# First loads of a gated linear-attention and SwiGLU kernel: two x tiles on two queues, the halves of wk on the other queue each

## The chip, the core and the metric

The kernel runs on one core of a Trainium2 chip. TensorE (PE) does the matmuls, VectorE (DVE), ScalarE (ACT) and GpSimd (POOL) the elementwise work, and SyncE (SP) issues DMAs. ACT can issue DMAs as well. The metric is the device time of one execution in microseconds, lower is better.

## What is computed

Two branches of one input x (2048 tokens, 512 features, bf16) are mixed by a gate. Branch A is linear attention with 32 heads of 16 features, without a causal mask; branch B is a SwiGLU block with 1376 hidden features. Cut to what matters:

```python
g = sigmoid((x * gate_w).sum(-1, keepdims=True))
# branch A
q, k, v = split_heads(x @ wqkv)
pq, pk = phi(q), phi(k)          # phi(t) = where(t > 0, t + 1, exp(t)) + 1e-6
kv  = einsum("bhsd,bhse->bhde", pk, v)
z   = einsum("bhsd->bhd", pk)
a   = (pq @ kv) / (pq @ z + 1e-6) @ wo
# branch B
b   = (silu(x @ w1) * (x @ w3)) @ w2
out = g * a + (1 - g) * b
```

## The kernel before

The tokens are cut into 16 tiles of 128 (`t`), and four tiles make a block of 512 (`tb`). The feature dimension of 512 is cut into four chunks of 128 (`kc`). All weights and all of x stay on chip: `x_sb` holds x with tokens on the partitions, `xT` holds it transposed (features on the partitions), and `wk_sb`, `wq_sb`, `wv_sb`, `w1_sb`, `w3_sb`, `w2_sb`, `wo_sb` hold the weights.

The work comes in this order on TensorE, and the order is written out by hand (line 152 puts TensorE under manual scheduling, so its instructions run in the order of the program text):

1. Warm matmuls (`emit_warm`, lines 160 to 167): six with 512 columns and three with 128, on constants, whose result is not used.
2. Transposes of x tiles 0 and 1 (`emit_xT`, lines 171 to 183): four 128x128 transposes a tile. DVE copies the first two of a tile out of PSUM (line 181), ACT the other two (line 183).
3. The k projection of the first block (lines 376 to 385). Its sixteen matmuls (line 186) run in a fixed order. The first six are, as (kc, t): (0,0), (1,0), (0,1), (1,1), (2,0), (3,0). So the first four need only chunks 0 and 1 of wk, and the fifth is the first to need chunks 2 and 3. Then come (2,1), (3,1), and tiles 2 and 3.
4. For the tiles from 4 on, the k projection alternates with `emit_xp` (line 206), which accumulates x^T phi(k) over all tokens.
5. The q projection of block 0, the products that fold kv and wo into one matrix `W_sb`, and then, block by block, the SwiGLU matmuls (`emit_ffn`), the next block's q projection and remainder, and the output (`emit_out`).

xT of tiles 0 and 1 is made on TensorE as said. xT of all other tiles comes by transposing DMAs from DRAM (lines 89 and 93).

The DMAs are issued in the order of the text on their queue. SP's queue (`dq`) carries nearly all of them: x tiles 0 and 1 (line 84), the second half of wk (line 86), the transposing load of tiles 2 and 3 (line 89), then the rest of xT and x, and the weights in the order of use (lines 92 to 114). ACT's queue carries one: the first half of wk (line 85). After it ACT runs a one-element `Exp` (line 88, tile `pre`), ahead of which the table of activation functions is loaded. Scheduling of ACT, DVE, POOL and SP is left to the framework.

x tiles 0 and 1 are loaded in one DMA of 256 KB whose partition p takes rows 2p and 2p + 1 of x (2 KB in one piece). So tile 0 holds the even rows of the first 256 and tile 1 the odd ones. The sums over tokens do not depend on the order, and the output rows of these two tiles are stored with the same stride (`out_first`, lines 83 and 371).

The lines that matter here:

```python
dq.dma_start(out=x_sb[:, 0:TF, :], in_=x_first)
nc.scalar.dma_start(out=wk_sb[:, 0:2, :], in_=wqkv_r[:, 0:2, D : 2 * D])
dq.dma_start(out=wk_sb[:, 2:4, :], in_=wqkv_r[:, 2:4, D : 2 * D])
pre = consts.tile([1, 1], FP32, name="pre")
nc.scalar.activation(out=pre[:], in_=nc.const_aps.tensor(0.0, [1, 1], FP32), func=ACT.Exp)
```

Of the kernel before, what the change touches and what calls it, by code (L numbers as in the profile page):

```python
# [8 lines left out]
ACT = mybir.ActivationFunctionType  # L9
ALU = mybir.AluOpType  # L10
AX = mybir.AxisListType
ENG = mybir.EngineType
FP32 = mybir.dt.float32
# [4 lines left out]
def kernel(  # L18
# [12 lines left out]
    nc = tc.nc  # L31
    P = nc.NUM_PARTITIONS

    Bb, S, D = A_x.shape
# [5 lines left out]
    TB = 512  # L40
    NTB = S // TB
    TPB = TB // P
    FC = F // P
    FR = F - FC * P
    FM = FC * P
# [3 lines left out]
    x2d = A_x.flatten_outer_dims()  # L49
    out2d = out.flatten_outer_dims()  # L50
# [13 lines left out]
    x_sb = consts.tile([P, NT, D], BF16, name="x_sb")  # L64
    xT = consts.tile([P, KC, S], BF16, name="xT")
    wk_sb = consts.tile([P, KC, D], BF16, name="wk_sb")
# [5 lines left out]
    w2_sb = consts.tile([P, FC, D], BF16, name="w2_sb")  # L72
# [3 lines left out]
    wqkv_r = A_wqkv.rearrange("(kc d) n -> d kc n", d=P)  # L76
    w1_r = B_w1.rearrange("(kc d) f -> d kc f", d=P)
    w3_r = B_w3.rearrange("(kc d) f -> d kc f", d=P)
    x_r = x2d.rearrange("(t p) d -> p t d", p=P)
    dq = nc.sync  # L80
    TF = 2
    x_first = x2d[0 : TF * P, :].rearrange("(p j) d -> p j d", j=TF)
    out_first = out2d[0 : TF * P, :].rearrange("(p j) d -> j p d", j=TF)
    dq.dma_start(out=x_sb[:, 0:TF, :], in_=x_first)
    nc.scalar.dma_start(out=wk_sb[:, 0:2, :], in_=wqkv_r[:, 0:2, D : 2 * D])
    dq.dma_start(out=wk_sb[:, 2:4, :], in_=wqkv_r[:, 2:4, D : 2 * D])
    pre = consts.tile([1, 1], FP32, name="pre")
    nc.scalar.activation(out=pre[:], in_=nc.const_aps.tensor(0.0, [1, 1], FP32), func=ACT.Exp)
    dq.dma_start(
        out=xT[:, :, TF * P : TB], in_=x2d[TF * P : TB, :], transpose=True  # L90
    )
    for tb in range(1, NTB):
        dq.dma_start(
            out=xT[:, :, tb * TB : (tb + 1) * TB], in_=x2d[tb * TB : (tb + 1) * TB, :],
# [7 lines left out]
    with nc.allow_non_contiguous_dma(reason="one gate weight per partition and chunk"):  # L102
        dq.dma_start(
            out=wr_sb[:, :, 2 * FR : NR], in_=gate_w.rearrange("(kc d o) -> d kc o", d=P, o=1)
# [3 lines left out]
        dq.dma_start(out=w1_sb[:, :, fsl], in_=w1_r[:, :, fsl])  # L108
        dq.dma_start(out=w3_sb[:, :, fsl], in_=w3_r[:, :, fsl])
    dq.dma_start(out=wo_sb[:], in_=A_wo.rearrange("(kc d) n -> d kc n", d=P))  # L110
    w2_r = B_w2[0:FM, :].rearrange("(fc f) d -> f fc d", f=P)
    for fcs in (slice(0, FC // 2), slice(FC // 2, FC)):
        dq.dma_start(out=w2_sb[:, fcs, :], in_=w2_r[:, fcs, :])
    dq.dma_start(out=w2r_sb[:FR, :], in_=B_w2[FM:F, :])

    pk_sb = consts.tile([P, NT, D], BF16, name="pk_sb")
# [5 lines left out]
        out=bm, in_=bm, pattern=[[-Dh, HPC], [0, Dh]], compare_op=ALU.is_ge, fill=0.0,  # L122
# [3 lines left out]
        out=bm, in_=bm, pattern=[[Dh, HPC], [0, Dh]], compare_op=ALU.is_ge, fill=0.0,  # L126
# [33 lines left out]
    def emit_warm(*widths):  # L160
        warm = psX.tile([P, TB], FP32, tag="XP3", name="warm")
        for n in widths:
            nc.tensor.matmul(  # L163
                warm[:, 0:n], lhsT=warm_l, rhs=warm_r[:, 0:n], start=True, stop=True
            )

    emit_warm(TB, TB, TB, TB, TB, TB, P, P, P)

    st = {}

# [163 lines left out]
    def emit_out(tb, tt):  # L334
        t = tb * TPB + tt
        tsl = slice(tt * P, (tt + 1) * P)

        if t < NT - 1:
            parts = [(0, D, True)]
        else:  # L340
            h, q3 = D // 2, 3 * D // 4
            parts = [(0, h, True), (h, q3, False), (q3, D, True)]
        o_out = work.tile([P, D], BF16, tag="o_out", name="o_out")
        lo = 0
        for i, (a, b, store) in enumerate(parts):
            o_ps = psX.tile([P, b - a], FP32, tag=f"XP{2 + (tt + i) % 2}", name="o_ps")
            for c in range(KC):
                nc.tensor.matmul(  # L348
                    o_ps[:], lhsT=st[tb, "pqT"][:, c, tsl], rhs=W_sb[:, c, a:b],
                    start=(c == 0), stop=False,  # L350
                )
            nc.tensor.matmul(  # L352
                o_ps[:], lhsT=st[tb, "hTr"][:FR, tsl], rhs=w2r_sb[:FR, a:b],
                start=False, stop=False,
            )
            for fc in range(FC):
                nc.tensor.matmul(  # L357
                    o_ps[:], lhsT=st[tb, "hT"][:, fc, tsl], rhs=w2_sb[:, fc, a:b],
                    start=False, stop=(fc == FC - 1),
                )  # L360
            if i < 2:
                nc.scalar.activation(  # L362
                    out=o_out[:, a:b], in_=o_ps[:], func=ACT.Copy, scale=omg[:, t : t + 1]
                )
            else:
                nc.vector.tensor_scalar(  # L366
                    out=o_out[:, a:b], in0=o_ps[:], scalar1=omg[:, t : t + 1], scalar2=None,
                    op0=ALU.mult,
                )
            if store:  # L370
                rows = out_first[t] if t < TF else out2d[t * P : (t + 1) * P, :]
                nc.sync.dma_start(out=rows[:, lo:b], in_=o_out[:, lo:b])
                lo = b


# [39 lines left out]
    for c in range(KC):  # L415
# [7 lines left out]
        out=kvT_sb[:], in0=kvT_ps[:],  # L423
# [21 lines left out]
    for tb in range(NTB):  # L445
        for fc in range(FC if tb == 0 else 0, FC):
            emit_ffn(tb, fc)
        nx = tb + 1
        for tt in range(TPB):
            if nx < NTB:  # L450
                emit_q(nx, tt, psX, "XP0")
                if tt % 2 == 0:
                    emit_rem(nx, tt // 2, psX, "XP1")
            emit_out(tb, tt)
            if nx < NTB:
                emit_den(nx, tt)
        if nx < NTB:
            emit_norm(nx)
# [30 lines left out]
```

## Time and profile before

| What | Value |
|---|---|
| Median of 4 runs | 179.52 us (179.37 to 180.15) |
| Profiled execution, its own time | 179.57 us |
| Its span, first to last instruction | 177.7 us |
| TensorE busy | 173.9 us, 98% of the span |
| First transpose of x starts | 3.93 us |
| First k matmul starts | 4.75 us |
| Last matmul starts | 174.61 us |

A profile is of one execution. Times in it count from the first instruction, so the span is a little shorter than the execution's own time; here 1.87 us lie around it. "PE" is a matmul, "PEld" a weight load that overlaps it. "SPq" and "ACTq" are DMAs being issued by SP and ACT: the length given is that of the issue, and the time to landing is told apart, in the view of the DMA issues. What stands in square brackets at the end of a timeline line is the engine's idle time before it and what ended that.

### The profile page before, as it was taken

To read this page: it belongs to the slowest core of one execution; us is meant where nothing else is said; L and a number is where in the kernel's file an instruction comes from. 1 tells how busy PE (TensorE), PEld (TensorE's weight loads), DVE (VectorE), ACT (ScalarE), POOL (GpSimd) and SP (SyncE) were. 2 spreads that over 40 slices of the span, in tenths; PEclk is the share of its full clock that TensorE was granted. 3 is DMA by queue.
4 is the path that set the end of the run, shared out by engine and by line. 5 is a ranking of instruction groups with operands and counts; after the bars stand their busy time and mean duration, and the time that the engine had idled before them with its cause. 6 is when DMAs were issued, how large, how long until landed. Compare 5 with 4: busy or idle time off the path is not lost.

```text
span 177.7 us, 2469 instructions
## 1 busy us (share of the span) xinstructions
PE 173.9 (98%) x884; PEld 84.0 (47%) x884; DVE 117.9 (66%) x203; ACT 66.0 (37%) x124; POOL 63.3 (36%) x71
## 2 busy tenths in 40 slices
PE   8999999999999999999999999999999999999993
PEld 3444444474444444444454544444545444444463
DVE  0596857898998637498776366978754668775000
ACT  3634224466443434333244333243434323241211
POOL 5197655967262323262003232710032328000000
PEclk9999999999999999999999999999999999999999
DMA  5999999921014011124000111230002022200011
GB/s 170 236 293 239 246 339 363 348 78 28 9 30 90 3 41 38 40 59 89 0 0 11 39 35 37 70 79 6 0 7 66 7 70 59 59 0 0 30 41 51
DMA packets 30252, 15.14 MB, mean 85 GB/s; under 512 B 20672, under 2 KB 30112, under 8 KB 30240
## 3 DMA queue, kind: packets, MB, share of 16 engines
q1 hardware_dynamic: 29968, 14.72, 30.6%
q10 hardware_dynamic: 272, 0.26, 0.4%
q8 instruction: 7, 0.11, 0.3%
q14 instruction: 5, 0.04, 0.1%
HBM read 8.42 MB, written 2.10 MB: 59 GB/s over the span
## 4 chain that ended last, share of the span: by engine, by line
PE 98%; DVE 0%; issue 0%; DVEq 0%
PE o_ps L357 19%; PE gate_ps L312 19%; PE up_ps L320 19%; PE o_ps L348 8%; PE XP L206 8%; PE q_ps L219 8%; PE k_ps L186 6%; PE r_ps L243 3%; PE o_ps L352 2%; PE k L186 2%; PE warm L163 2%; PE xTp L176 1%; PE kvT_ps L418 1%; PE W_ps L440 0%; DVE o_out L366 0%; PE z_ps L431 0%
## 5 line engine op out<-in xcount | busy, mean ns | idle before, releaser
L312 PE MATMUL gate_ps<-xT,w_sb 128*128 128x512 bf16 x160 | 41.1, 379 | 0.0
L320 PE MATMUL up_ps<-xT,w_sb 128*128 128x512 bf16 x160 | 41.1, 379 | 0.0
L227 POOL TENSOR_TENSOR qz<-pq,z_sb 128x512 f32<-128x512 bf16 x16 | 18.5, 1165 | 59.6 <-DVE pq L147 58.4
L325 ACT ACTIVATE th<-gate_ps 128x512 bf16<-128x512 f32 x40 | 23.9, 597 | 37.9 <-PE gate_ps L312 37.5
L357 PE MATMUL o_ps<-w_sb,hT 128*128 128x512 bf16 (+2 forms) x180 | 37.5, 355 | 0.0
L327 DVE SCALAR_TENSOR_TENSOR gs<-th,gate_ps 128x512 bf16<-128x512 bf16 x40 | 27.3, 683 | 5.6 <-ACT th L325 5.3
L330 DVE TENSOR_TENSOR hT<-up_ps,gs 128x512 bf16<-128x512 f32 x40 | 27.7, 691 | 3.8
L144 DVE TENSOR_SCALAR phi_m<-phi_e 128x512 bf16<-128x512 bf16 x32 | 14.2, 442 | 21.3 <-ACT phi_e L142 21.2
L357 PEld LDWEIGHTS <-hT 128*128 128x128 bf16 x180 | 16.8, 97 | 17.9
L320 PEld LDWEIGHTS <-w_sb 128*128 128x128 bf16 x160 | 15.7, 98 | 18.9
L312 PEld LDWEIGHTS <-w_sb 128*128 128x128 bf16 x160 | 15.6, 98 | 18.6
L362 ACT ACTIVATE o_out<-o_ps,omg 128x512 bf16<-128x512 f32 (+2 forms) x17 | 11.2, 657 | 30.4 <-PE o_ps L357 30.4
L292 POOL TENSOR_TENSOR pqn<-pq,rden 128x512 bf16<-128x512 bf16 x16 | 16.6, 1058 | 14.0 <-DVE rden L285 11.7
L196 POOL TENSOR_TENSOR pks<-pks,pk_sb 128x512 f32<-128x512 f32 x15 | 17.4, 1162 | 7.3 <-DVE pk_sb L147 6.7
L348 PE MATMUL o_ps<-W_sb,pqT 128*128 128x512 bf16 (+2 forms) x72 | 16.8, 355 | 0.0
L230 DVE TENSOR_REDUCE den<-qz 128x32 f32<-128x512 f32 x16 | 11.0, 685 | 8.6 <-POOL qz L227 8.5
L219 PE MATMUL q_ps<-wq_sb,xT 128*128 128x512 bf16 x64 | 16.4, 379 | 0.0
L206 PE MATMUL XP<-pk_sb,x_sb 128*128 128x512 bf16 x64 | 16.3, 379 | 0.0
L142 ACT ACTIVATE phi_e<-k_ps 128x512 bf16<-128x512 f32 x12 | 7.2, 597 | 14.4 <-PE k_ps L186 14.4
L142 ACT ACTIVATE phi_e<-q_ps 128x512 bf16<-128x512 f32 x16 | 9.6, 598 | 7.8 <-PE q_ps L219 7.8
L186 PE MATMUL k_ps<-wk_sb,xT 128*128 128x512 bf16 x48 | 12.3, 379 | 0.0
L147 DVE SCALAR_TENSOR_TENSOR pq<-q_ps,phi_m 128x512 bf16<-128x512 f32 x16 | 11.1, 691 | 0.5
(59 smaller groups left out, 117.7 us busy)
## 6 DMA issues: line engine op xcount, KB each, us to landing
w_sb<-in_B_w_dram SPq DMA_DIRECT2D x6, 640.0 KB, 8.4
out_dram<-o_out SPq DMA_DIRECT2D x15, 128.0 KB, 1.9
x_sb<-in_A_x_dram SPq DMA_DIRECT2D x2, 512.0 KB, 4.2
x_sb<-in_A_x_dram SPq DMA_DIRECT2D x1, 768.0 KB, 5.1
wq_sb<-in_A_wqkv_dram SPq DMA_DIRECT2D x1, 512.0 KB, 6.1
wv_sb<-in_A_wqkv_dram SPq DMA_DIRECT2D x1, 512.0 KB, 6.7
wo_sb<-in_A_wo_dram SPq DMA_DIRECT2D x1, 512.0 KB, 10.0
wk_sb<-in_A_wqkv_dram ACTq DMA_DIRECT2D x1, 256.0 KB, 3.6
```

Source lines behind the costliest of these rows:

```text
L186: nc.tensor.matmul(k_ps[:], lhsT=xT[:, kc, t * P : (t + 1) * P], rhs=wk_sb[:, kc, :], start=(kc == 0), stop=(kc == KC - 1),)
L196: nc.gpsimd.tensor_add(pks[:], pks[:], pk_sb[:, t, :])
L206: nc.tensor.matmul(XP_ps[dc][:], lhsT=x_sb[:, t, dc * P : (dc + 1) * P], rhs=pk_sb[:, t, :], start=(t == 0), stop=(t == NT - 1),)
L219: nc.tensor.matmul(q_ps[:], lhsT=xT[:, kc, ts_tok], rhs=wq_sb[:, kc, :], start=(kc == 0), stop=(kc == KC - 1),)
L227: nc.gpsimd.tensor_tensor(out=qz[:], in0=st[tb, "pq"][:, tt, :], in1=z_sb[:], op=ALU.mult)
L312: nc.tensor.matmul(gate_ps[:], lhsT=w1_sb[:, kc, fsl], rhs=xT[:, kc, tok_sl], start=(kc == 0), stop=(kc == KC - 1),)
L320: nc.tensor.matmul(up_ps[:], lhsT=w3_sb[:, kc, fsl], rhs=xT[:, kc, tok_sl], start=(kc == 0), stop=(kc == KC - 1),)
L325: nc.scalar.activation(out=th[:], in_=gate_ps[:], func=ACT.Tanh, scale=0.5)
L327: nc.vector.scalar_tensor_tensor(out=gs[:], in0=th[:], scalar=1.0, in1=gate_ps[:], op0=ALU.add, op1=ALU.mult)
L330: nc.vector.tensor_tensor(out=st[tb, "hT"][:, fc, :], in0=up_ps[:], in1=gs[:], op=ALU.mult)
L348: nc.tensor.matmul(o_ps[:], lhsT=st[tb, "pqT"][:, c, tsl], rhs=W_sb[:, c, a:b], start=(c == 0), stop=False,)
L357: nc.tensor.matmul(o_ps[:], lhsT=st[tb, "hT"][:, fc, tsl], rhs=w2_sb[:, fc, a:b], start=False, stop=(fc == FC - 1),)
```

## The change

x tiles 0 and 1 become two loads of 128 KB, tile 0 on SP's queue and tile 1 on ACT's; tile t holds rows 128t to 128t + 127 again. The first half of wk moves to SP's queue, behind x tile 0. The second half of wk moves to ACT's queue and stands behind the one-element `Exp`, and so behind the load of its table; these few instructions are put under manual scheduling for ACT, so that they keep this order. Two of the three short warm matmuls go. w2 is loaded by one DMA instead of two. The outputs of tiles 0 and 1 are stored to contiguous rows, like all others.

```diff
-    x_first = x2d[0 : TF * P, :].rearrange("(p j) d -> p j d", j=TF)
-    out_first = out2d[0 : TF * P, :].rearrange("(p j) d -> j p d", j=TF)
-    dq.dma_start(out=x_sb[:, 0:TF, :], in_=x_first)
-    nc.scalar.dma_start(out=wk_sb[:, 0:2, :], in_=wqkv_r[:, 0:2, D : 2 * D])
-    dq.dma_start(out=wk_sb[:, 2:4, :], in_=wqkv_r[:, 2:4, D : 2 * D])
     pre = consts.tile([1, 1], FP32, name="pre")
-    nc.scalar.activation(out=pre[:], in_=nc.const_aps.tensor(0.0, [1, 1], FP32), func=ACT.Exp)
+    with tc.manual_schedule(engines={ENG.Activation}):
+        dq.dma_start(out=x_sb[:, 0, :], in_=x_r[:, 0, :])
+        nc.scalar.dma_start(out=x_sb[:, 1, :], in_=x_r[:, 1, :])
+        dq.dma_start(out=wk_sb[:, 0:2, :], in_=wqkv_r[:, 0:2, D : 2 * D])
+        nc.scalar.activation(
+            out=pre[:], in_=nc.const_aps.tensor(0.0, [1, 1], FP32), func=ACT.Exp
+        )
+        nc.scalar.dma_start(out=wk_sb[:, 2:4, :], in_=wqkv_r[:, 2:4, D : 2 * D])
...
-    w2_r = B_w2[0:FM, :].rearrange("(fc f) d -> f fc d", f=P)
-    for fcs in (slice(0, FC // 2), slice(FC // 2, FC)):
-        dq.dma_start(out=w2_sb[:, fcs, :], in_=w2_r[:, fcs, :])
+    dq.dma_start(out=w2_sb[:], in_=B_w2[0:FM, :].rearrange("(fc f) d -> f fc d", f=P))
...
-    emit_warm(TB, TB, TB, TB, TB, TB, P, P, P)
+    emit_warm(TB, TB, TB, TB, TB, TB, P)
...
-                rows = out_first[t] if t < TF else out2d[t * P : (t + 1) * P, :]
-                nc.sync.dma_start(out=rows[:, lo:b], in_=o_out[:, lo:b])
+                nc.sync.dma_start(
+                    out=out2d[t * P : (t + 1) * P, lo:b], in_=o_out[:, lo:b]
+                )
```

## Prediction

> **What bounds the kernel now.** I read the page's busy shares first, then the chain that ended last, then the timeline of the first 12 us in narrow windows, then the DMA issues, and last when each loaded tile is first used.
>
> ```profile
> span 177.7 us, 2469 instructions
> PE 173.9 (98%) x884; PEld 84.0 (47%) x884; DVE 117.9 (66%) x203; ACT 66.0 (37%) x124; POOL 63.3 (36%) x71
> ...
> PE 98%; DVE 0%; issue 0%; DVEq 0%
> ```
>
> TensorE is busy for 173.9 of 177.7 us and is the whole chain. The chain in order of time has no gap from 3.93 us to the last matmul. So an edit counts only if it moves the moment at which the dense stream begins, or opens a hole in it; DVE, ACT and POOL have room everywhere. The last matmul starts at 174.61 us, and what follows (one eviction, one store) is not touched. All of the decision lies in the first six microseconds:
>
> ```profile
> 0.80 0.45 ACTq L85 DMA_DIRECT2D wk_sb<-in_A_wqkv_dram  x1
> 0.81 0.40 SPq L84 DMA_DIRECT2D x_sb<-in_A_x_dram  x1
> 0.84 3.04 PE L163 MATMUL warm<-const-bfloat16-1.0 128*128 128x512 bf16 x9 [0.84 <-PEq L473]
> 1.27 0.41 SPq L86 DMA_DIRECT2D wk_sb<-in_A_wqkv_dram  x1
> 1.28 1.28 ACT L88 ACT_TABLE_LOAD   x1 [1.28 <-PEq L473]
> 1.73 1.32 SPq L89 DMA_TRANSPOSE xT<-in_A_x_dram  x1
> 2.58 0.20 ACT L88 ACTIVATE pre<-const-float32-0.0 1x1 f32<-1x1 f32 x1
> 3.92 0.77 PEld L176 LDWEIGHTS <-x_sb 128*128 128x128 bf16 x8 [0.31 <-DMA x_sb<-in_A_x_dram]
> 4.57 0.79 ACT L183 ACTIVATE xT<-xTp 128x256 bf16<-128x256 bf16 x2 [1.79 <-PE xTp L176]
> 4.75 3.64 PE L186 MATMUL k<-wk_sb,xT 128*128 128x512 bf16 x16
> ```
>
> The columns are start and length in us. Three things are to be seen. The transposes wait for x: it lands 3.1 us after its issue (0.81 + 3.1 = 3.9). The warm matmuls were done before that: the last one starts at 3.57. And the sixteen k matmuls begin once the transposes are through, at 4.75. The DMA view gives the two halves of wk:
>
> ```profile
> wk_sb<-in_A_wqkv_dram ACTq DMA_DIRECT2D x1, 256.0 KB, 3.6
> x_sb<-in_A_x_dram SPq DMA_DIRECT2D x1, 256.0 KB, 3.1
> wk_sb<-in_A_wqkv_dram SPq DMA_DIRECT2D x1, 256.0 KB, 4.0
> ```
>
> So half one (kc 0, 1) lands at 0.80 + 3.6 = 4.4, half two (kc 2, 3) at 1.27 + 4.0 = 5.27. By the order written out, half one is first needed by k matmul 1 (4.75) and half two by k matmul 5, which starts at 5.64: slack 0.35 and 0.37 us.
>
> **The clock of the start.** TensorE is slow here. The 512-column warm matmuls start 0.43 us apart and the transposes 0.107 us apart; later 512-column matmuls start 0.216 us apart.
>
> ```profile
> 4.75 0.41 PE L186 MATMUL k<-wk_sb,xT 128*128 128x512 bf16 x1
> ...
> 4.75 0.62 PE L186 MATMUL k<-wk_sb,xT 128*128 128x512 bf16 x2
> ```
>
> Both lines are narrow windows: the first holds k matmul 1 alone (0.41 us, the settled ones take 0.379), the second 1 and 2, so 2 starts at 5.00, 0.243 after 1. With c us of the 0.243 at the slow pace, c/0.427 + (0.243 - c)/0.216 = 1 gives c = 0.055: the fast pace begins at about 4.81 us. (The granted clock of the rows reads 1.00 all along; the spacing is what shows it.) I take 4.81 as fixed in time, since the changed kernel keeps TensorE busy from 0.84 on as well.
>
> **The change, part by part.**
>
> Warm matmuls: nine become seven, two of 128 columns go. The seventh starts at 3.360, so the transposes can begin at 3.360 + 0.107 = 3.47, if x tile 0 is there; before they began at 3.93. At most 0.46 us is won.
>
> x as two 128 KB loads, one on each queue, issued where x and wk half one are issued now (0.81 and 0.80). No row shows a 128 KB load. Bounds: 1.9 us (the 128 KB stores of the DMA view) and 3.6 us (the ACT queue's load). Tile 0 lands between 2.7 and 4.4, tile 1 likewise. I take 3.1 us or a little less for tile 0 and 3.1 for tile 1, because together they are the same 256 KB that took 3.1 now, with nothing ahead of them. Tile 0 is needed at 3.47, tile 1 four transposes later, at 3.47 + 4 x 0.107 = 3.90, which is 0.80 + 3.1. The eight transposes then end at 4.32. At the far bound (tile 1 at 4.4) the transposes end near 4.8, k matmul 3 is at 5.26 and not 5.21, and the part costs 0.05 us.
>
> The Trainium skill, "DMA: Bandwidth & Descriptors", section "Issuing engines are not separate DMA queues", speaks against this part: loads from two queues run on the same DMA engines, and only issue time is saved. The busy DMA share of 0.99 to 1.10 between 2.75 and 4.25 us agrees. Taken strictly, both tiles land when the one load did, the transposes start at 3.93 and this part is worth nothing: 179.57.
>
> wk half one on the sync queue at 1.27, where half two is now. It comes behind the 256 KB of x, as it does in effect now (both were issued at 0.80, and x landed first), so I keep its landing at 4.4 to 4.45. Bounds: 3.1 and 4.0 us after 1.27, that is 4.4 and 5.27. k matmul 1 starts at about 4.47 and not 4.75.
>
> Then the sum. From 4.47 to 4.81 it runs at 0.427: 0.34/0.427 = 0.80 of it is done, the rest takes 0.20 x 0.216 = 0.04. k matmul 2 starts at 4.85 and not 5.00: **0.15 us won**. The slow clock takes the rest of the 0.28. Matmul 5 starts at 4.85 + 3 x 0.216 = 5.50.
>
> wk half two on ACT, written behind the table load and the dummy activation. It has to land by 5.50 for the gain, and by 5.64 for no loss. Its issue time is the open point. If ACT issues it while the table load runs (from 1.28 on), landing is 1.3 to 1.5 plus 4.0 = 5.3 to 5.5, and nothing stalls. If it waits until the activation starts or ends (2.58, 2.78), landing is 2.58 + 3.6 = 6.2 to 2.78 + 4.0 = 6.8, and TensorE, whose order is fixed by hand, stands still. So this part costs between 0 and 1.15 us against before. I take the early issue: the activation starts 0.01 us after the table load ends, so it had been handed on already while the table load ran, and what stands behind it in ACT's stream is then free to issue. Behind the issue on ACT stand the copies of xT (line 183), first at about 4.1 in the new kernel; even the late issue, 0.45 us long, is over by 3.23.
>
> The skill's "Perfetto Trace Analysis", section "Sequencer Loop", says the same of a sequencer (engine instructions are pushed into a queue); no ACT DMA behind a running instruction is in this trace.
>
> The rest is hidden. On SP the first transposing load stays third (1.73); its tile lands at 6.23, and k matmul 9, which needs it, moves from 6.51 to 6.36, so 0.13 us of slack is left. w2 in one load instead of two: the halves are issued at 25.0 and 26.8 and land within 10.6 us, before 38 us, and w2 is first used at 59.1, a cover of some 20 us; SP has one issue less. The stores of output tiles 0 and 1 are 128 KB as before, near 63 and 66 us, and TensorE does not wait for them. x tiles 0 and 1 hold other rows, in the same shapes.
>
> Sum: profiled execution 179.57 (span 177.7 and 1.87 around it) less 0.15 gives 179.4. The median shown is 179.52, 0.05 lower, which I leave aside.
>
> **Rivals.**
> 1. Nothing won, or a little lost: both x tiles at 3.9, or wk half one late. If half one lands at 4.7 to 5.0, matmul 1 starts there and not at 4.75; matmul 3 was held by the copy of tile 1 until 5.21. Cost 0 to 0.25 us: 179.55 to 179.8. For it: half two, issued at 1.27 on this queue, took 4.0 us. Against it: that one had 512 KB ahead of it.
> 2. wk half two is late (slower). One mechanism: the second ACT issue waits for the table load. From an issue later than about 1.65 (5.64 - 4.0) every microsecond goes straight into the stream, because k matmuls 5 to 16 follow in fixed order. Price 0.55 to 1.15: 180.1 to 180.7, middle 180.4. For it: its place in ACT's order. Against it: the 0.01 us gap.
> 3. The full gain: the fast clock comes earlier along with the work and half one is in time. Then all of the 0.46 is kept: 179.1. Against it: the clock has changed in time, not in work, in the one trace there is.
>
> **How the numbers follow.** A difference of 0.3% (0.54 us) is about what a measurement of this kernel can tell from no change. Forecast 179.4 with 0.50; rival 1 with 0.15; rival 2 with 0.25; rival 3 with 0.10. Forecast and rival 1 lie within 0.3%; rival 2 lies above it except at its lowest end; rival 3 lies inside by 0.08 us, so I split it, half faster. The four runs of before alone go from 179.37 to 180.15, and I add 0.04 to faster and nothing to slower for such scatter: faster 0.09, same 0.66, slower 0.25. The range runs from 179.05 (rival 3 inside) to 180.4 (half of rival 2), which leaves out some 0.17.
>
> **What would show it.** In the changed profile: transposes near 3.47 and k matmul 1 near 4.47; k matmul 2 near 4.85; no hole before k matmul 5; ACT's second DMA issue before 2.5 us. A second ACT issue at 2.6 or later with a hole before matmul 5 is rival 2; transposes at 3.9 are rival 1; fast spacing well before 4.8 is rival 3. A hole later than 8 us would mean that I overlooked a load.

## The result, and the profile after

The change made the kernel slower. The median is 180.14 us (44 executions) against 179.62 us (63 executions of the kernel before, the earlier four among them); the ratio is 1.0033, with a 95% interval of 1.0021 to 1.0044, that is 0.4 to 0.8 us. Ratios here leave out slow executions, those more than 1.5% above the fastest of their kernel. The fastest executions are 0.46 us apart (179.57 and 179.11). Five of the 44 took 181.9 to 182.5 us; none of the 63 took more than 180.42.

The profiled execution of the changed kernel has a span of 178.4 us. This is the timeline of its first microseconds (start, length, engine, line, operation; in brackets the engine's idle time before it and what ended that):

```profile
0.80 0.41 ACTq L85 DMA_DIRECT2D x_sb<-in_A_x_dram  x1
...
0.81 0.40 SPq L84 DMA_DIRECT2D x_sb<-in_A_x_dram  x1
...
1.24 1.28 ACT L87 ACT_TABLE_LOAD   x1 [1.24 <-PEq L474]
1.26 0.42 SPq L86 DMA_DIRECT2D wk_sb<-in_A_wqkv_dram  x1
1.30 0.43 ACTq L90 DMA_DIRECT2D wk_sb<-in_A_wqkv_dram  x1
...
3.49 0.78 PE L176 MATMUL xTp<-ident,x_sb 128*128 128x128 bf16 x8
...
5.32 3.61 PE L186 MATMUL k<-wk_sb,xT 128*128 128x512 bf16 x16 [1.04 <-DMA wk_sb<-in_A_wqkv_dram]
```

The transposes did move forward, from 3.93 to 3.49. But the k matmuls moved back, from 4.75 to 5.32, and the bracket names what they waited for: wk. The second half of wk, which stands behind the table load in ACT's program, was issued at 1.30, while that load was still running (1.24 to 2.52), and so only 0.04 us after the first half on SP. The DMA view (last column: us from issue to landing) gives the landings:

```profile
wk_sb<-in_A_wqkv_dram SPq DMA_DIRECT2D x1, 256.0 KB, 4.0
wk_sb<-in_A_wqkv_dram ACTq DMA_DIRECT2D x1, 256.0 KB, 4.2
...
x_sb<-in_A_x_dram ACTq DMA_DIRECT2D x1, 128.0 KB, 2.8
x_sb<-in_A_x_dram SPq DMA_DIRECT2D x1, 128.0 KB, 2.6
```

Half one now lands at 1.26 + 4.01 = 5.27 us, and half two 0.25 us after it, at 5.52. In the kernel before, the trace has the two landings at 4.45 and 5.25. So the half that is needed first lost 0.8 us. The chain that ended last, in order of time, now begins with that load (start, length, what):

```profile
1.26 4.01 DMA wk_sb<-in_A_wqkv_dram
5.32 3.61 PE k L186 x16
```

One more view shows what the DMA engines did meanwhile. These are the same microsecond of both kernels, first before and then after (length; busy time and instructions of PE, PEld, DVE, ACT, POOL; granted clock; DMA share; GB/s):

```profile
4.25:5.25 1.00, 1.00 (x10) 0.74 (x9) 0.58 (x2) 0.65 (x2) 0.00 (x0) 1.00 1.20 291
```

```profile
4.25:5.25 1.00, 0.02 (x1) 0.10 (x1) 0.24 (x1) 0.49 (x2) 0.00 (x0) 1.00 1.19 271
```

TensorE went from full to empty, and the DMA engines were as busy as before and moved nearly as much (271 against 291 GB/s). The bytes came at much the same rate. They came in another order.

The trace shows the order itself: it lists each packet (a piece of 1 KB for wk) with its queue, start and length. In the kernel before, half two's first packet started at 3.75 us, when 84% of half one's 256 packets were done. In the changed kernel it started at 3.22, when 11% were, and from 3.5 to 4.5 us SP's queue moved 151 KB of half one while ACT's moved 198 KB of half two.

From the first XP matmul (line 206) on, nothing differs: the last matmul of the kernel starts 166.38 us after it in both profiles, to 0.01 us. So the price can be read at one place, the start of that matmul: 8.235 before, 8.765 after, 0.53 us later.

### The profile page after: what moved, and what is told of

It reads as the page before. It is cut to its first block, busy times and chain, and to the rows that moved or that the text cites. A ratio compares the mean times of both kernels' runs of the same rounds, so it can differ in the third digit from the quotient of the medians.

```text
span 178.4 us, 2465 instructions
## 1 busy us (share of the span) xinstructions
PE 173.5 (97%) x882; PEld 83.6 (47%) x882; DVE 117.9 (66%) x203; ACT 65.9 (37%) x124; POOL 63.2 (35%) x71
## 4 chain that ended last, share of the span: by engine, by line
PE 95%; DMA 2%; SPq 0%; DVE 0%; issue 0%; DVEq 0%
PE o_ps L357 19%; PE up_ps L320 19%; PE gate_ps L312 19%; PE o_ps L348 8%; PE XP L206 8%; PE q_ps L219 8%; PE k_ps L186 6%; PE r_ps L243 3%; DMA wk_sb<-in_A_wqkv_dram 2%; PE k L186 2%; PE o_ps L352 2%; PE kvT_ps L419 1%; PE W_ps L441 0%; SPq L84 0%; DVE o_out L366 0%; PE z_ps L432 0%
```

## The experiments

Three readings were to be told apart. **S (sharing):** the halves of wk were now issued on two queues at the same time, ran side by side on the DMA engines, and the first became nearly as late as the second. **Q (queue):** half one is late because it stands second on SP's queue, behind x tile 0. **W:** the fewer warm matmuls or the single load of w2 are what costs.

All landings and starts are in us from the first instruction. Half one and half two are the halves of wk; "T" is the transposing load of tiles 2 and 3; k1 is the start of the first k matmul, XP that of the first XP matmul. "Fast from" is the start of the first stretch of full clock in the trace's clock records; from there on 512-column matmuls start 0.216 us apart and no longer 0.427. (e1's trace has no such record; there the time is worked out from the spacing.) All of these are from the one profiled execution of each run. Times are medians of all executions; the ratio is to executions of the kernel before on the same chip, whose medians were 179.70 (e1 to e4), 179.48 (e5 to e8) and 179.62 (f).

| Run | x landed | half one | half two | T | k1 | fast from | XP | time | ratio (95%) |
|---|---|---|---|---|---|---|---|---|---|
| before | 3.88 | 4.45 | 5.25 | 6.23 | 4.75 | 4.80 | 8.24 | 179.62 | |
| after | 3.44, 3.60 | 5.27 | 5.52 | 6.50 | 5.32 | 3.87 | 8.77 | 180.14 | 1.0033 (1.0021 to 1.0044) |
| e1_half2_sync | 3.83, 3.63 | 4.39 | 6.23 | 7.28 | 4.71 | 6.55 | 9.07 | 180.24 | 1.0030 (1.0011 to 1.0048) |
| e2_half2_waits | 3.44, 3.63 | 6.21 | 9.51 | 9.47 | 6.25 | 4.55, then 14.79 | 14.62 | 184.38 | 1.0228 (1.0184 to 1.0273) |
| e3_swapped | 3.60, 3.77 | 5.65 | 5.41 | 6.59 | 5.69 | 4.90 | 9.14 | 182.55 | 1.0138 (1.0096 to 1.0179) |
| e4_side_edits | 3.66 | 4.35 | 5.47 | 6.52 | 4.44 | 3.87 | 8.30 | 179.67 | 0.9989 (0.9972 to 1.0006) |
| e5_quarter | 3.51, 3.34 | 5.02 | 4.36, 5.53 | 6.69 | 5.06 | 5.96 | 8.94 | 180.57 | 1.0050 (1.0026 to 1.0074) |
| e6_fill | 3.34, 3.52 | 6.04 | 5.36 | 7.00 | 6.08 | 4.90 | 9.53 | 180.48 | 1.0042 (1.0023 to 1.0061) |
| e7_split_T | 3.68 | 4.36 | 5.20 | 5.68, 6.50 | 4.56 | 6.01 | 8.73 | 180.38 | 1.0043 (1.0020 to 1.0066) |
| e8_both_act | 3.55 | 4.25 | 5.16 | 6.15 | 4.34 | 3.68 | 7.93 | 179.95 | 1.0018 (1.0000 to 1.0035) |
| f1_x_1kb | 4.38 | 4.71 | 5.54 | 6.45 | 5.25 | 6.76 | 9.45 | 179.85 | 1.0028 (1.0010 to 1.0046) |
| f2_after_again | 3.49, 3.65 | 5.99 | 6.25 | 7.19 | 6.03 | 4.38 | 9.48 | 180.30 | 1.0063 (1.0033 to 1.0093) |
| f3_before_again | 3.74 | 4.31 | 5.19 | 6.18 | 4.61 | 4.64 | 8.08 | 179.36 | one execution |
| f4_after_fill | 3.48, 3.65 | 4.97 | 5.44 | 6.47 | 5.20 | 5.87 | 8.99 | 180.59 | 1.0052 (1.0033 to 1.0070) |

**e1_half2_sync: half two behind half one on SP.**

```diff
         dq.dma_start(out=wk_sb[:, 0:2, :], in_=wqkv_r[:, 0:2, D : 2 * D])
+        dq.dma_start(out=wk_sb[:, 2:4, :], in_=wqkv_r[:, 2:4, D : 2 * D])
...
-        nc.scalar.dma_start(out=wk_sb[:, 2:4, :], in_=wqkv_r[:, 2:4, D : 2 * D])
```

> The changed kernel, but wk's second half goes on SP's queue right behind the first half, so the two halves no longer run on two queues. Theory S (sharing: in the changed kernel the second half was issued at 1.30 us, ran beside the first half on the same DMA engines and made it late): half one lands at 4.4 to 4.5 us and not 5.27, half two at 5.2 to 5.4, k matmul 1 starts near 4.5 and k matmul 5 near 5.4; time 0.1 to 0.4 us below before, 179.2 to 179.5. Theory Q (queue: half one is late because it now stands second on SP's queue, behind x tile 0): half one still lands near 5.3 and the time stays at that of the changed kernel, 180.1. Theory W (the warm matmuls or w2 are what costs): 180.1 as well, with half one early.

Half one landed at 4.39 and k1 came at 4.71, so S holds and Q falls: half one's place behind x tile 0 was the same. (k1 was not earlier because the x tiles landed only at 3.63 and 3.83 here, and the transposes, at the slow pace, ran until 4.7.) The rest was a miss: half two landed at 6.23, not by 5.4, and the time stayed at 180.24. The timeline and the stages of the profile show what went on (the second fence's columns are those of the stages above):

```profile
1.27 0.44 SPq L86 DMA_DIRECT2D wk_sb<-in_A_wqkv_dram  x1
1.75 0.46 SPq L87 DMA_DIRECT2D wk_sb<-in_A_wqkv_dram  x1
2.26 1.68 SPq L91 DMA_TRANSPOSE xT<-in_A_x_dram  x1
...
4.71 4.53 PE L186 MATMUL k<-wk_sb,xT 128*128 128x512 bf16 x16
```

```profile
4.50:5.50 1.00, 1.00 (x6) 0.50 (x5) 0.40 (x2) 0.77 (x2) 0.00 (x0) 1.00 1.58 185
5.50:6.50 1.00, 1.00 (x4) 0.39 (x3) 0.00 (x0) 0.00 (x0) 0.00 (x0) 1.00 0.83 162
```

The transposing load is now issued fourth, at 2.26 instead of 1.73, and while it ran beside the rest of half two the engines moved 185 and 162 GB/s, against 278 and 273 in the same stages before. T landed at 7.28 instead of 6.23, and the matmul that needs it, the ninth, started at 7.34 instead of 6.51. So the repair of one wait prepared another. No matmul waited for T in this profile, since TensorE was slow until 6.55 and arrived at its ninth matmul no earlier than T. In an execution with an early fast pace it would have had to wait, but none such was traced; how much of the time of e1 is T and how much the clock is not shown.

**e2_half2_waits: half two really behind the table load.** The dummy activation writes one element of wk's second half, which the load then overwrites, so the load has to wait.

```diff
         nc.scalar.activation(
-            out=pre[:], in_=nc.const_aps.tensor(0.0, [1, 1], FP32), func=ACT.Exp
+            out=wk_sb[0:1, 2, 0:1], in_=nc.const_aps.tensor(0.0, [1, 1], FP32), func=ACT.Exp
         )
```

> The changed kernel, but the one-element activation writes into the second half of wk, which the load then overwrites; so the load must wait for the activation and is really behind the table load. Theory S: ACT issues it near 2.75 us, half one has the DMA engines to itself until then and lands at 4.4 to 4.6, k matmul 1 near 4.5; half two lands 2.8 to 4.2 us after its issue, at 5.5 to 6.9, and k matmul 5 starts then (before: 5.64). Time from 0.1 below to 1.2 above before, 179.5 to 180.8, and the hole stands before k matmul 5, not before k matmul 1. Theory Q: half one lands near 5.3 all the same, and the hole before k matmul 1 stays; 180.1 or more.

The issue came where expected, at 2.77. Neither half landed where S expected it. The timeline of TensorE, and three stages of the profile:

```profile
3.49 1.03 PE L176 MATMUL xTp<-ident,x_sb 128*128 128x128 bf16 x8
6.25 1.02 PE L186 MATMUL k<-wk_sb,xT 128*128 128x512 bf16 x4 [1.73 <-DMA wk_sb<-in_A_wqkv_dram]
9.55 5.28 PE L186 MATMUL k<-wk_sb,xT 128*128 128x512 bf16 x12 [2.27 <-DMA wk_sb<-in_A_wqkv_dram]
```

```profile
4.55:7.96 3.41, 1.02 (x4) 0.38 (x4) 0.09 (x1) 0.38 (x1) 0.00 (x0) 1.00 1.15 114
7.96:14.78 6.82, 5.23 (x13) 1.93 (x13) 2.83 (x6) 1.79 (x3) 1.76 (x2) 0.50 1.12 245
14.78:20.00 5.22, 5.17 (x25) 2.35 (x24) 4.15 (x7) 1.79 (x3) 3.40 (x3) 1.00 1.13 238
```

Two things are to be seen. First, half two now met the transposing load instead of half one, on another queue, and the two obstructed each other: 114 GB/s over 3.4 us, T at 9.47, half two at 9.51. Even half one, whose last packet had ended at 3.85, as early as in the kernel before, got its last completion counts only at 6.21. Why the two loads hinder each other so much is not shown. Second, the holes seem to cost the clock: after the stretch of 3.41 us in which TensorE was busy for 1.02, the granted clock (third column from the right) falls to 0.50 from 7.96 to 14.78 us, and the k matmuls run at 0.427 us again. The profiled execution was the longest of six (186.08 us, the others 182.2 to 184.7), so its numbers show what can happen and not the usual price; no other execution of e2 was traced.

**e3_swapped: the halves of wk on each other's queue.**

```diff
-        dq.dma_start(out=wk_sb[:, 0:2, :], in_=wqkv_r[:, 0:2, D : 2 * D])
+        nc.scalar.dma_start(out=wk_sb[:, 0:2, :], in_=wqkv_r[:, 0:2, D : 2 * D])
+        dq.dma_start(out=wk_sb[:, 2:4, :], in_=wqkv_r[:, 2:4, D : 2 * D])
...
-        nc.scalar.dma_start(out=wk_sb[:, 2:4, :], in_=wqkv_r[:, 2:4, D : 2 * D])
```

> The changed kernel with the halves of wk on each other's queue: half one on ACT behind x tile 1, half two on SP behind x tile 0, both issued near 1.25 us. Theory S: they still run side by side, both land at 5.1 to 5.5, k matmul 1 waits until then; 180.0 to 180.2. Theory Q: half one on ACT lands at 4.4, k matmul 1 near 4.5, 179.3 to 179.5.

```profile
wk_sb<-in_A_wqkv_dram ACTq DMA_DIRECT2D x1, 256.0 KB, 4.4
wk_sb<-in_A_wqkv_dram SPq DMA_DIRECT2D x1, 256.0 KB, 4.1
```

```profile
5.69 3.61 PE L186 MATMUL k<-wk_sb,xT 128*128 128x512 bf16 x16 [1.01 <-DMA wk_sb<-in_A_wqkv_dram]
```

S again. Half one, on ACT from 1.24, landed at 5.65, 0.15 us later than S allowed; half two, on SP from 1.27, at 5.41; k1 started at 5.69. Here the halves stand on the queues on which the kernel before has them, and yet they hinder each other. What differs from before is x: with x split over both queues, both halves stand second on their queue and come up together; before, half two stood behind the whole of x. The time was a miss (180.0 to 180.2 was expected): two executions took 180.7 us, the other four 182.4 to 182.9.

**e4_side_edits: the kernel before, with the fewer warm matmuls and the single load of w2.**

```diff
-    emit_warm(TB, TB, TB, TB, TB, TB, P, P, P)
+    emit_warm(TB, TB, TB, TB, TB, TB, P)
...
-    for fcs in (slice(0, FC // 2), slice(FC // 2, FC)):
-        dq.dma_start(out=w2_sb[:, fcs, :], in_=w2_r[:, fcs, :])
+    dq.dma_start(out=w2_sb[:], in_=B_w2[0:FM, :].rearrange("(fc f) d -> f fc d", f=P))
```

> The kernel before with two parts of the change alone: seven warm matmuls instead of nine, and w2 in one load. The loads of x and wk are those of before. Theories S and Q: as before within 0.2 us, 179.4 to 179.8, transposes still at 3.9. Theory W: 0.4 us or more above before, by a later rise of the TensorE pace or a hole after 30 us.

```profile
4.44 4.03 PE L184 MATMUL k<-wk_sb,xT 128*128 128x512 bf16 x16
8.30 1.03 PE L204 MATMUL XP<-pk_sb,x_sb 128*128 128x512 bf16 x4
```

No difference that shows, ratio 0.9989 with 1 inside the interval; W falls. (Lines are two earlier here. The transposes started at 3.71, and not at 3.9 as expected, as x landed at 3.66.) This profile is also the fair partner of the changed kernel's: TensorE became fast at 3.87 in both. The first XP matmul starts at 8.30 here and 8.77 there: 0.46 us.

**e5_quarter: half as much beside half one.** Chunk 2 of wk on SP behind half one, only chunk 3 (128 KB) on ACT.

```diff
         dq.dma_start(out=wk_sb[:, 0:2, :], in_=wqkv_r[:, 0:2, D : 2 * D])
+        dq.dma_start(out=wk_sb[:, 2:3, :], in_=wqkv_r[:, 2:3, D : 2 * D])
...
-        nc.scalar.dma_start(out=wk_sb[:, 2:4, :], in_=wqkv_r[:, 2:4, D : 2 * D])
+        nc.scalar.dma_start(out=wk_sb[:, 3:4, :], in_=wqkv_r[:, 3:4, D : 2 * D])
```

> The changed kernel with half as much on the other queue: chunk 2 of wk goes on SP behind half one, only chunk 3 (128 KB instead of 256 KB) stays on ACT beside half one. Theory S (what is issued early on the other queue shares the DMA engines with half one): a dose, so half one lands between the 4.39 us of the run with nothing beside it and the 5.27 us of the changed kernel, at 4.6 to 5.0, and k matmul 1 starts there. Rival (any load on ACT at that time costs the same, whatever its size): 5.2 to 5.4. The first transposing load is issued 0.4 us later on SP than in the changed kernel, lands at 7.0 or later, and holds k matmul 9 back; so the time is no better than the changed kernel's: 180.0 to 180.4.

With 0, 128 and 256 KB beside it, half one landed at 4.39, 5.02 and 5.27 in these profiles. The order is that of a dose, but the changed kernel's other two profiles have 5.99 and 4.97 for 256 KB, so the steps between are not resolved by single profiles. What stands is that the small load, needed last, came first (4.36). Half one's 5.02 is at the end of what S expected (4.6 to 5.0). T at 6.69 was earlier than expected, and the time, 180.57, above what was expected (180.0 to 180.4). Two of the twelve executions took 182.19 and 182.75.

**e6_fill: e3_swapped with three matmuls in the idle stretch.** Their result is not used.

```diff
     emit_xT(1)
+    emit_warm(TB, TB, TB, tag="XP0")
```

> The kernel with the halves of wk swapped between the queues (its runs: 180.7 twice, 182.4 to 182.9 four times), with three more 512-column matmuls whose result is not used between the transposes and k matmul 1, in the stretch in which TensorE stood idle for 1.1 us. Theory C (clock: the runs near 182.7 are those in which the idle stretch kept TensorE at the slow pace for one more period): no run above 181.3, median 180.5 to 181.1. Rival (a DMA lands 2 us late in these runs): the runs near 182.7 stay, four in six or so.

Nine executions, 179.95 to 180.95, none near 182.7, although half one landed later still in its profile (6.04). So C: the long executions of e3_swapped look like a matter of TensorE's pace after an idle stretch, not of a DMA. (e3 and e6 ran on different chips, and e6's profile still has 0.66 us of idle time before k1.) **f4_after_fill** did the same to the changed kernel, with two matmuls:

> The changed kernel with two more 512-column matmuls without use between the transposes and k matmul 1, in its idle stretch of one microsecond. The loads are those of the changed kernel, so half one still lands near 5.3 and the time stays 0.3 to 0.7 above before. Theory C (clock): the few runs near 182 (5 of 44 of the changed kernel) are gone, none above 181.3. Rival (those runs are a late DMA): one or two of a dozen remain near 182.

Ten executions, 179.83 to 180.98, none near 182, against 8 of 56 of the changed kernel (5 of 44 and 3 of 12 in f2_after_again). The median did not fall, as half one was still late; the two matmuls cost something themselves when TensorE is slow. (Were the share still 8 in 56, ten executions without one would come up one time in five; it is e6_fill that carries the point, nine without where four of six had it.)

No long execution was traced, so the clock is argued here and not seen. Three figures of the record speak for it. Every execution above 181.5 us, but for those of e2, belongs to a kernel whose profile has TensorE idle for 0.5 to 1.5 us before k1 (the changed kernel, e3, e5). One more stretch of 3.41 us, as in e2, at the slow pace would cost about 3.41 x (1 - 0.216/0.427) = 1.7 us, an estimate; e3's long executions took 1.7 to 2.2 more than its short ones. And the mean granted clock of the long ones is 0.997 to 1.00, where e2's executions with a later fall of the clock have 0.98 to 0.99: so it would be the first rise that came late, not a fall after it. The records do not count the slow pace ahead of the first rise.

**e7_split_T: the kernel before with the first transposing load cut in two.**

```diff
-    dq.dma_start(
-        out=xT[:, :, TF * P : TB], in_=x2d[TF * P : TB, :], transpose=True
-    )
+    for t in range(TF, TPB):
+        dq.dma_start(
+            out=xT[:, :, t * P : (t + 1) * P], in_=x2d[t * P : (t + 1) * P, :], transpose=True
+        )
```

> The kernel before with its first transposing load (tiles 2 and 3, line 89) cut in two of one tile each. If tiles 2 and 3, needed from k matmul 9 on, are what the start waits for once the TensorE pace is fast early, tile 2 lands at 5.7 to 6.1 instead of 6.23 to 6.52 and the time falls by 0 to 0.4 us against before, 179.2 to 179.6. If the issue of one more transposing load on SP costs more than that, tile 3 and what follows land later, and the time is 0 to 0.6 above before.

Tile 2 landed earlier, at 5.68, and tile 3 at 6.50; the time went up, as the second half of the expectation has it. The profile shows one hole further on: the XP matmul at 12.41 us starts 0.44 us after the matmul before it, instead of 0.216. Its weight load waited for the load of x tiles 2 to 7, which is issued behind the transposing loads and landed at 12.37 instead of 11.04. This hole, 0.24 us from the first XP matmul to the last (166.61 instead of 166.38), is a part of the price; the rest is not separated.

**e8_both_act: the kernel before with half two on ACT behind half one.**

```diff
-    dq.dma_start(out=wk_sb[:, 2:4, :], in_=wqkv_r[:, 2:4, D : 2 * D])
+    nc.scalar.dma_start(out=wk_sb[:, 2:4, :], in_=wqkv_r[:, 2:4, D : 2 * D])
```

> The kernel before with half two of wk on ACT too, straight behind half one on the same queue; SP then issues the transposing load second, at 1.27 us instead of 1.73. Theory S: half two no longer competes with anything but the transposing load does; that load now runs beside the halves of wk, so half one or half two or both land later than before (4.45, 5.25), by 0.3 us or more, and the time is 0.3 to 2 us above before, as in the run in which half two ran beside it. Rival (only the two halves hinder each other): half one at 4.45, half two at 5.2, tiles 2 and 3 no later than 6.3, time as before or 0.2 below.

S as it was put here was wrong, and the rival right on the landings: 4.25, 5.16, and T at 6.15. Two loads of wk on one queue follow each other, and the transposing load, though issued at 1.26 on the other queue, disturbed neither. It was next on its queue once x was through at 3.15, but the trace has its first packet (256 bytes) only at 4.33, when 82% of half two were done. So it is not enough that two loads are issued together, nor that both are next on their queues. Why T held back is not shown: in the other profiles its first packet started at 4.23 to 4.52, in e2 at 3.67. The time did not follow: 179.95, at or a little above before. The profiled execution, with TensorE fast from 3.68, was the quickest of the twelve (179.31).

**f1_x_1kb: the kernel before with x in 256 pieces of 1 KB instead of 128 of 2 KB.**

```diff
-    dq.dma_start(out=x_sb[:, 0:TF, :], in_=x_first)
+    dq.dma_start(out=x_sb[:, 0:TF, :], in_=x_r[:, 0:TF, :])
...
-                rows = out_first[t] if t < TF else out2d[t * P : (t + 1) * P, :]
+                rows = out2d[t * P : (t + 1) * P, :]
```

> The kernel before, its x tiles 0 and 1 still in one load on SP, but each row of 1 KB on its own partition (256 pieces of 1 KB instead of 128 of 2 KB). It asks why x and half one of wk, issued together on two queues, did not hinder each other before. Theory P (piece size: fewer, larger pieces put x ahead): x and half one now run side by side, x lands at 4.0 to 4.6 us instead of 3.6 to 3.9, and the time is 0.2 to 0.6 above before. Theory N (the order of the loads, not the pieces): x at 3.6 to 3.9, half one at 4.3 to 4.5, time as before within 0.2.

```profile
wk_sb<-in_A_wqkv_dram ACTq DMA_DIRECT2D x1, 256.0 KB, 3.9
x_sb<-in_A_x_dram SPq DMA_DIRECT2D x1, 256.0 KB, 3.6
```

P. Same bytes, same issue times, same queues, and x landed 0.5 to 0.7 us later (4.38 against 3.88, 3.74 and 3.66) and half one 0.3 to 0.4 later. In the packet records, 46% of half one were done when 90% of x were; in the other three profiles it was 2 to 11%. So the kernel before owed its good order in part to the 2 KB pieces: they put x ahead of half one on the other queue. The changed kernel gives these up as well, but its x tiles land early all the same, since only they compete.

**f2_after_again and f3_before_again: both kernels unchanged, for second profiles.**

> The changed kernel once more, unchanged, for a second profile of it beside others on the same chip. If half one's late landing belongs to the kernel and not to the one profiled execution, half one lands at 5.0 to 5.5 us and k matmul 1 starts there; time 0.3 to 0.8 above before. If it was chance, half one lands near 4.4.

> The kernel before once more, unchanged, for a second profile. If the landings of its loads belong to the kernel, x lands at 3.5 to 3.9 us, half one at 4.2 to 4.6, half two at 5.1 to 5.5, tiles 2 and 3 at 6.2 to 6.6; the moment at which the TensorE pace doubles may be another than 4.8.

```profile
6.03 3.61 PE L186 MATMUL k<-wk_sb,xT 128*128 128x512 bf16 x16 [1.49 <-DMA wk_sb<-in_A_wqkv_dram]
```

This is the k line of f2_after_again: half one was later still, at 5.99. Over three profiles with these loads it landed at 4.97, 5.27 and 5.99; with the loads of the kernel before (before, f3, e4) at 4.45, 4.31 and 4.35. The two groups do not touch.

The packets show that the lateness has two parts:

| Profile | 90% of half one's packets done | last packet done | half one landed |
|---|---|---|---|
| before, f3, e4 | 3.79, 3.74, 3.85 | 4.07, 3.93, 4.00 | 4.45, 4.31, 4.35 |
| e1 | 3.67 | 3.94 | 4.39 |
| after, f2, f4 | 4.17, 4.17, 4.18 | 4.86, 5.40, 4.60 | 5.27, 5.99, 4.97 |

The first nine tenths are 0.3 to 0.4 us late in all three profiles of the changed loads, before T's first packet (4.39 to 4.45). That part is the sharing with half two. What differs from profile to profile is the last tenth: in f2 a few packets of both halves stayed behind, and from 5.25 to 5.75 us the engines moved only 25 GB/s. T's packets were under way by then. Whether T held the last packets up was not tested.

## Why the prediction was wrong

**The step that failed** is "wk half one on the sync queue": I kept its landing at 4.4 to 4.45 because x stands ahead of it as before. It landed 0.5 to 1.5 us later. The prediction asked of half two only when it would land itself, and took the early issue as the good case, in which "nothing stalls". The early issue came, at 1.30, and it is what did the harm, to the other half: without it on ACT's queue (e1) half one landed at 4.39. With half one late, k matmul 1 started at 5.32, and not at 4.47 as the sum has it. The late issue that I feared as rival 2 (e2_half2_waits) is worse, and for more than its place after 5.64: in the one profile it runs into the transposing load, and half two lands at 9.51, not at 6.2 to 6.8. I had the price of being late at 0.55 to 1.15 us; it was over 2.

The place of the loss was named in rival 1, half one at 4.7 to 5.0, with 0 to 0.25 us. Its price was too small by half. The prediction's own far bound for this landing was 5.27, from the 4.0 us of a load with 512 KB ahead of it, and rival 1 did not go that far; f2's 5.99 lies beyond the bound too. The completion counts show the same as the packets. Each load raises its semaphore by sixteen counts, and it has landed with the last. Half one's came in from 4.14 to 4.45 us before. After, fourteen came from 4.21 to 4.87, and the last two at 5.25 and 5.27; in f2 fourteen came by 4.81, and the last two at 5.79 and 5.99. (Rival 1 also has k matmul 3 held by a copy until 5.21. It was not held: it starts 0.216 us after matmul 2, at the fast pace.)

The Trainium skill, "DMA: Bandwidth & Descriptors", section "Issuing engines are not separate DMA queues", says that DMAs from different engines interleave on the same DMA engines. I weighed it for the two x tiles, where it makes no difference of note, since both are needed. It bore on the two halves of wk, where one is needed first; e1, e3 and the packets show it there.

**Right were these steps.** The transposes start with the end of the warm matmuls (3.49; 3.47 forecast); the x tiles land in time, at 3.44 and 3.60, earlier than the 3.9 that I took; the second ACT load is not held by the table load; w2 and the warm matmuls cost nothing that shows (e4), nor do the stores of tiles 0 and 1, which lie within the 166.38 us told next; and TensorE's order is so tight that the delay at the start goes to the end undiminished (166.38 us from the first XP matmul to the last in all profiles but e2's and e7's).

**Half right: the clock.** I took the change of pace at 4.81 as fixed in time. In fourteen profiles it came anywhere from 3.68 to 6.76 us, with the first matmul always at 0.84. It is no property of either kernel: the kernel before has 4.80 and 4.64, its like e4 has 3.87, the changed kernel has 3.87 and 4.38. So the 0.15 us that I computed was one draw. It can account for much of the spread of the kernel before (179.1 to 180.4): with k1 at 4.75, a rise at 6.76 costs about (6.76 - 4.75) x (1 - 0.216/0.427) = 1.0 us, an estimate. And in one respect the two seem to be tied: the idle stretch before k1 in the changed kernel (1.04 and 1.49 us) went with about two more in 8 of 56 executions, and with the fillers there were none. The skill's "TensorE: Matmul & The Clock Gate", section "What's actually happening", says that activity is judged in windows of 3.41 us that run free of the kernel. e2's stretches agree: fast for 3.41 us, slow for 6.83, which is twice that.

**The account.** At equal clock (after against e4) the change costs 0.46 us: k1 is 0.88 us later (5.32 against 4.44), but e4 then loses 0.2 us in each of two places, before its fifth matmul (half two landed at 5.47) and before its ninth (T landed at 6.52), where the changed kernel, later by then, does not wait. The fastest executions differ by the same 0.46. The rest of the measured difference, up to 0.8 at the end of the interval, would lie in the long executions and in chance in the clock; their shares were not separated. That sharing makes half one late is shown; no run shows the time coming back when half one is in time (e1: 180.24, where half two and T came later instead).

**What stays open:** what holds up the last tenth of half one, from 4.60 to 5.40 between profiles of the same loads; why e8, with the best landings of all, was not faster in its twelve executions; and why the transposing load is hindered in e1 and e2 but not in e8. No version here beats the kernel before.

## What to carry to other kernels

When a stage needs several loads in order, do not ask of each only when it is issued; ask what comes up on the other queue at the same time. Here two loads in 1 KB pieces, next on their two queues, shared the engines, and the one needed first landed nearly with the second. The order was kept where the later load stood behind something: on the same queue, or behind a big first load on the other one. And a load that is moved out of the way of one (e1, e2) has to be followed to the next one it meets, here the transposing load.

## What the runs showed of the hardware

- A DMA behind an activation and a table load on ACT is issued while the table load runs (1.30 us, load from 1.24 to 2.52). Where its data made it wait for the activation, it was issued at 2.77 (e2).
- A load of 256 KB in 128 pieces of 2 KB had its way before another queue's load; in 256 pieces of 1 KB it shared (x at 3.66 to 3.88 against 4.38).
- A transposing load beside an ordinary load on another queue went with a far lower rate than two ordinary loads side by side had: 114 GB/s over 3.4 us in the longest execution of e2, against 365 in the changed kernel from 3.75 to 4.25 us and 273 from 5.5 to 6.5 us in the kernel before, where transposing loads ran alone. Beside the rest of an ordinary load on the same queue it did so to a lesser degree (185 and 162 GB/s in e1). In e8 it did not: its first packet came at 4.33, when the other queue's loads were nearly through.
- A load's last counts can come long after its data: in e2 half one's last packet ended at 3.85 and its last count came at 6.21, beside the transposing load; in the kernel before the two lie 0.38 us apart.
- TensorE's first change of pace is not tied to the first matmul: 2.8 to 5.9 us after it, from execution to execution.
